# Attention, soft MoE and feed-forward on one core: a written order for SyncE's DMAs, and the maxima one step after the scores

## The chip, the cores and the metric

The kernel runs on one core of one Trainium2 chip. Its engines are TensorE (PE in the profile; PEld is its weight load), VectorE (DVE), ScalarE (ACT), GpSimd (POOL) and SyncE (SP), which issues nearly all DMAs (SPq in the rows). Each engine works through its own list of instructions in order, and they meet at semaphores. The metric is the device time of one execution in microseconds, and the time shown for a kernel is the median of its runs.

## The reference

Three layers follow one another; the change touches the first.

```python
scores = scale * np.matmul(q, k.transpose(0, 1, 3, 2))      # q, k, v: 8 x 8 x 576 x 64
scores = np.where(block_i >= block_j, scores, -1e9)         # causal by blocks of 64
scores = scores - np.max(scores, axis=-1, keepdims=True)
attn = np.exp(scores); attn = attn / (attn.sum(-1, keepdims=True) + 1e-9)
x = np.matmul(attn, v)                                      # then reshaped to 4608 x 512
logits = x @ phi                                            # soft MoE, 8 experts x 4 slots
slot_out[e] = np.maximum(slot_input[e] @ w1[e], 0) @ w2[e]  # slot_input: softmax over tokens
y = softmax(logits, axis=1) @ slot_out
out = np.maximum(y @ w_in, 0) ** 2 @ w_out                  # feed-forward, 4608 x 512
```

## The kernel before

Attention goes over 8 batches of 8 heads. Two heads make a pair, four pairs a batch, so there are 32 pairs, numbered n = 0 to 31 through all batches (bn is the batch, jn the pair in it). The work is pipelined over pairs, and `pair(n)` writes one step of that pipeline:

- `split(n + 3)` scales q and k of the pair three ahead into 16-bit high and low parts. ScalarE makes the high part (`high`), VectorE the low one (`low`). `prep_k` sends both parts of k through a DMA transpose to `s1` (in the rows s<-ka); q's high part is turned by TensorE (`turn_q`) and copied to `t1`; q's low part goes to `qb`.
- `maxpass(n + 2)` computes the scores of the pair two ahead in one pass for their row maxima alone: seven chunks, each a few matmuls into a PSUM tile ps_max and a VectorE reduction to pm. Its last part, `fin`, joins them, writes the maxima into `qb` (the last instruction is L535) and sends `qb` through a DMA transpose to `t2` (t<-qb, L540).
- `s2copy(n + 1)` is a DMA inside the core: it copies the upper half of s1 to a second tile s2 (s<-s, L952). There are two such tiles, used in turn.
- `scores(n)` computes the scores proper in seven chunks into ps_sc: each with s1 and t1, then with s2 and t2, which brings in the low part and the maxima. ScalarE takes the exponential of each chunk (p, L594; the last, small chunk gives pd, L576). The end of a pair, below, is the matmul of its last chunk (L574).
- `pv(n - 1)` multiplies the exponentials of the pair before with v, and sums them. GpSimd adds for it (ss).
- `aux` holds `scale`, the sums of squares that give the scaling: ScalarE squares k and q of a pair (junk, L380), TensorE sums over partitions (ps_ssq, L387), VectorE works out the scales. In odd pairs it does this for the pairs four and five ahead.
- `work` holds the soft MoE's part for the batch before (logits, running maxima, tokens), and `decq` the decoding of w_in, which comes as 64-bit numbers: 16 blocks, each loaded to raw (`load_in`), one ScalarE and four VectorE instructions a block (L185 to L206).

A pair is written in eight slots. Before, slot i holds chunk i of the scores and, right behind it, chunk i of the maxima; slot 0 holds also the pair's first steps of split, chunks 5 and 6 of the maxima and the output products.

DMA issues wait in a list `dq`, from which `loads(LR)`, with LR = 4, takes up to four in each slot. Loads of q and k come by pair (`load_pair`) for batches 0 and 1 and by batch (`load_batch`: first the small tails of k and q, then k, then q) after that; v by pair (`load_v`). `s2copy(n + 1)` is put at the head of `dq` in slot 2, and most loads at its head too:

```python
if i == 2 and n + 1 < N:
    dq.insert(0, lambda: s2copy(n + 1))
loads(LR)
```

In the whole of attention only TensorE keeps the order in which its instructions are written (`manual_schedule(engines={PE})`). On the other engines a scheduler orders them when the program is built, SyncE among them, so that the order of the DMAs is not that of `dq`.

Weights of the experts go into buffers that attention frees, by `wchunks`; the last of them only when attention ends. After attention come the experts and then the feed-forward.

Of the kernel before, what the change touches and what calls it, by code (L numbers as in the profile page):

```python
# [23 lines left out]
def tile_attn_soft_moe_ffn(  # L24
# [13 lines left out]
    B, H, S, D = q.shape  # L38
# [7 lines left out]
    NU = S // 128  # L46
# [38 lines left out]
    tin = tin_p.tile([128, KD, FF], F32, name="tin")  # L85
# [154 lines left out]
    def attention():  # L240
# [22 lines left out]
        N = B * NJ  # L263
# [40 lines left out]
        def load_v(n):  # L304
            b, j = divmod(n, NJ)
            t = v_tile(n)

            def main(hp):
                nc.sync.dma_start(
                    out=t[:, 0:NU, hp, :], in_=v[b][NJ * hp + j, 0:128 * NU, :].rearrange("(u p) d -> p u d", p=128)  # L310
                )

            def tail(hp):
                nc.sync.dma_start(
                    out=v_tail(b)[64 * hp:64 * hp + 64],
                    in_=v[b][NJ * hp:NJ * hp + NJ, 128 * NU:S, :].rearrange("j i d -> i j d"),
                )

            return [lambda: main(0)] + [lambda hp=hp: tail(hp) for hp in range(2) if j == 0] + [lambda: main(1)]

        def load_phi(hp):
            nc.sync.dma_start(
                out=phi2[64 * hp:64 * hp + 64, :, NSL * hp:NSL * hp + NSL],
                in_=phi.rearrange("(hp j p) s -> hp p j s", hp=2, p=64)[hp],
            )
# [25 lines left out]
        def load_batch(b):  # L351
            t = qk_tile(b)

            def main(nm, u):
                nc.sync.dma_start(
                    out=t[nm][:, 2 * u:2 * u + 2].rearrange("p x j d -> p (x j) d"),
                    in_=dict(q=q, k=k)[nm][b][:, 128 * u:128 * u + 128, :].rearrange("h p d -> p h d"),
                )

            def tail(nm, hp):  # L360
                nc.sync.dma_start(
                    out=t[nm][64 * hp:64 * hp + 64, 2 * NU],
                    in_=dict(q=q, k=k)[nm][b][NJ * hp:NJ * hp + NJ, 128 * NU:S, :].rearrange("j i d -> i j d"),
                )

            return [
                [lambda nm=nm, hp=hp: tail(nm, hp) for nm in "kq" for hp in range(2)],
                [lambda u=u: main("k", u) for u in range(NU)],
                [lambda u=u: main("q", u) for u in range(NU)],
            ]  # L370

        sc = {}
# [558 lines left out]
        raws = {}  # L931
# [8 lines left out]

        def decode_in(i):
            a, c = i % KD, i // KD
            return decode(dec_p, tin[:, a, 512 * c:512 * c + 512], raws.pop(i), 512)

        AHEAD, LR = 3, 4
        dq = load_pair(0, dict(q=nc.scalar)) + load_pair(1, dict(q=nc.scalar)) + load_pair(2) + load_pair(3)

        def loads(k):
            for _ in range(min(k, len(dq))):
                dq.pop(0)()  # L950
# [4 lines left out]
        with tc.manual_schedule(engines={mybir.EngineType.Activation}):  # L955
# [12 lines left out]
            m0 = maxpass(0)  # L968
            for f in m0[6:] + m0[:6] + [sp2[0], sp2[1], sp2[3]]:
                f()  # L970
        dq += load_v(0) + load_pair(4) + load_v(1) + load_pair(5) + [lambda hp=hp: load_phi(hp) for hp in range(2)]
        s3 = scale([AHEAD])
        m1 = maxpass(1)
        for i, f in enumerate(m1[6:] + m1[:6]):
# [7 lines left out]
        work, aux, decq, nraw = [], [], [], [0, 0]  # L982
        NRAW = KD * FF // 512
        ew = early = late_ = last = half = None
        bl = []
        def pair(n):
            nonlocal dq, work, aux, decq, bl, ew, early, late_, last, half
            bn, jn = divmod(n, NJ)
            m = maxpass(n + 2) if n + 2 < N else []
            s = scores(n) if n < N else []  # L990
            w = pv(n - 1) if n >= 1 else []
            if jn == 1:
                if bn >= 1:
                    work += batch(bn - 1)
                if bn + 1 == B:
                    while decq:
                        decq.pop(0)()
                    assert nraw[1] == NRAW, nraw
                    st_in.close()
                    wpools["a"] = w_st.enter_context(tc.tile_pool(name="wa", bufs=2, side="right"))  # L1000
                dq += wchunks({B - 2: 1, B - 1: 2}.get(bn, 0))

            elif jn == 2:
                if n == N - 2:
                    st_a.close()
                    wpools["e"] = w_st.enter_context(tc.tile_pool(name="we", bufs=1, side="right"))
                dq += wchunks({B - 2: 1, B - 1: 2}.get(bn, 0))
            elif jn == 3:
                if bn + 1 == B:
                    early, late_, last = batch(bn)  # L1010
                    work += early
                    st_b.close()
                    st_m.close()
                    wpools["m"] = w_st.enter_context(tc.tile_pool(name="wm", bufs=1, side="right"))
                    wpools["o"] = w_st.enter_context(tc.tile_pool(name="wo", bufs=2, side="right"))
                    dq += wchunks(3)
            elif n == N:
                work += late_
                st_c.close()
                wpools["n"] = w_st.enter_context(tc.tile_pool(name="wn", bufs=1, side="right"))  # L1020
                dq += wchunks(1)
            if nraw[1] < nraw[0] - 1 or NRAW == nraw[0] > nraw[1]:
                decq += decode_in(nraw[1])
                nraw[1] += 1
            if len(decq) <= 5 and 6 <= n and nraw[0] < NRAW:
                dq.append(lambda i=nraw[0]: load_in(i))
                nraw[0] += 1
            if n == 6:
                ew = wchunks(2)
            if n >= 7 and ew:  # L1030
                dq.append(ew.pop(0))
            if n + 2 < N:
                at = len(dq) if n < 4 else 0
                dq[at:at] = load_v(n + 2)
            if n == 0:
                dq += load_pair(6)
            if n == 1:
                dq[0:0] = load_pair(7)
            if jn == 1 and bn + 2 < B:
                bl = load_batch(bn + 2)  # L1040
                dq[len(load_pair(7)) if n == 1 else 0:0] = bl.pop(0) + bl.pop(0)
            if jn == 2 and bl:
                dq[0:0] = bl.pop(0)
            if n == 1:
                aux += scale([4]) + scale([5])
            if n == 2:
                aux += scale([6])
            if n % 2 and n > 1:
                ns = [i for i in (n + AHEAD + 1, n + AHEAD + 2) if i < N]
                aux += scale(ns, 2) if ns else []  # L1050
            sp = split(n + AHEAD) if n + AHEAD < N else []
            slot = {}

            def at_(i, *fs):
                slot.setdefault(i, []).extend(f for f in fs if f)

            get = lambda fs, i: fs[i] if i < len(fs) else None
            for i in range(7):
                at_(i, get(s, i), get(m, i) if i < 6 else None)
                if i == 0:  # L1060
                    early_ = sp and n != 1
                    at_(0, get(sp, 0) if early_ else None, get(m, 6), get(w, 0), get(sp, 1) if early_ else None, get(w, 1))
                    at_(0, get(sp, 2) if early_ else None)
            at_(3, get(w, 2))
            if n == 1:
                at_(3, sp[2])
                at_(4, sp[0])
                at_(7, sp[1], sp[3])
            else:
                at_(4, get(sp, 3))  # L1070
            for i in range(8):
                for f in slot.get(i, []):
                    f()
                if i == 2 and n + 1 < N:
                    dq.insert(0, lambda: s2copy(n + 1))
                loads(LR)
                f = aux.pop(0) if aux else None
                if f:
                    f()
                elif decq and i % 8:  # L1080
                    decq.pop(0)()
                for _ in range((i in (1, 3, 4, 6, 7)) if n < N - 3 else 1 if n < N - 1 else 2):
                    if work:
                        work.pop(0)()
            if n == N - AHEAD - 1:
                dq += wchunks(2)
            if n == N - 1:
                half = wchunk(14)
                dq += half[:1]
            if n >= 1:  # L1090
                P.pop(n - 1)
                T.pop(n - 1)
        with tc.manual_schedule(engines={mybir.EngineType.PE}):
            for n in range(N + 1):
                pair(n)
            nxt[0] += 1
            for f in dq + work + half[1:] + last:
                f()
# [585 lines left out]
```

## Time and profile before

| | |
|---|---|
| runs | 898.87, 904.22, 904.10 us; median 904.1 |
| the profiled execution | 901.67 us, its span 899.9 |
| before pair 0 ends | 0 to 39.95 us |
| pairs 1 to 31 | 39.95 to 435.2 us |
| rest of soft MoE, experts | 435.2 to about 505 us |
| feed-forward | about 505 to 899.9 us |
| DMA | 113.17 MB, 126 GB/s over the span |

All times in rows are of the profiled execution, counted from the start of its span; the 1.8 us between the span and its time lie outside. An engine's busy time says nothing by itself: it is compared with the length of its own stretch, pair by pair. The granted clock is a share of TensorE's full speed; it has two levels, 1.0 (2.4 GHz) and 0.5 (1.2 GHz), and a value between is a mean of the two over the stretch.

### The profile page before, as it was taken

To read this page: it belongs to the slowest core of one execution; us is meant where nothing else is said; L and a number is where in the kernel's file an instruction comes from. 1 tells how busy PE (TensorE), PEld (TensorE's weight loads), DVE (VectorE), ACT (ScalarE), POOL (GpSimd) and SP (SyncE) were. 2 spreads that over 40 slices of the span, in tenths; PEclk is the share of its full clock that TensorE was granted. 3 is DMA by queue.
4 is the path that set the end of the run, shared out by engine and by line. 5 is a ranking of instruction groups with operands and counts; after the bars stand their busy time and mean duration, and the time that the engine had idled before them with its cause. 6 is when DMAs were issued, how large, how long until landed. Compare 5 with 4: busy or idle time off the path is not lost.

```text
span 899.9 us, 21874 instructions
## 1 busy us (share of the span) xinstructions
PE 831.6 (92%) x8788; PEld 614.9 (68%) x8788; DVE 668.6 (74%) x1600; ACT 627.2 (70%) x1012; POOL 254.8 (28%) x394
## 2 busy tenths in 40 slices
PE   2778999898999989997997799999999999999998
PEld 1445667665676757664733344788888888888887
DVE  5755688888788878963551899888887888888881
ACT  5476788686878767753312689987878888888870
POOL 0234756557584846755200000000000000000000
PEclk9888999999999989999999799999999999999999
DMA  8899979879897969576999700100001000000002
GB/s 164 174 188 199 212 133 177 166 140 184 143 192 130 184 132 215 109 174 204 309 371 380 308 0 1 47 24 25 25 24 48 24 25 25 24 25 24 25 24 48
DMA packets 220486, 113.17 MB, mean 126 GB/s; under 512 B 192224, under 2 KB 194272, under 8 KB 220384
## 3 DMA queue, kind: packets, MB, share of 16 engines
q1 hardware_dynamic: 217728, 111.11, 53.7%
q8 instruction: 69, 1.13, 0.5%
q10 hardware_dynamic: 2656, 0.66, 0.4%
q14 instruction: 33, 0.27, 0.1%
HBM read 78.71 MB, written 9.44 MB: 98 GB/s over the span
## 4 chain that ended last, share of the span: by engine, by line
PE 64%; DMA 11%; POOL 8%; ACT 8%; DVE 4%; SPq 3%; issue 3%; ACTq 0%; DVEq 0%
PE ps_y L1498 14%; PE ps_x L1498 9%; PE ps_z L1498 9%; PE xm L629 6%; PE po L1520 4%; POOL ss L599 4%; DMA s<-s 4%; POOL ul L739 3%; PE ps_hb L1462 3%; PE ps_sc L556 3%; DMA wch<-in_moe_w_dram 3%; DMA ar_hi<-in_v_dram 2%; ACT p L594 2%; PE tl L640 2%; ACT t L465 1%
## 5 line engine op out<-in xcount | busy, mean ns | idle before, releaser
L1498 PEld LDWEIGHTS <-ah 128*128 128x128 f16 x1792 | 170.3, 98 | 21.9
L594 ACT ACTIVATE p<-ps_sc,es 128x512 f32<-128x512 f32 x192 | 128.9, 696 | 51.2 <-PE ps_sc L556 34.4
L491 DVE TENSOR_REDUCE pm<-ps_max 128x4 f32<-128x512 f32 x160 | 108.5, 683 | 58.2 <-PE ps_max L485 57.9
L1431 DVE TENSOR_TENSOR al<-a,ah 128x1024 f16<-128x1024 f32 (+1 forms) x128 | 138.5, 1124 | 16.7 <-ACT ah L1485 15.3
L599 POOL TENSOR_TENSOR ss<-p 128x384 f32<-128x384 f32 (+1 forms) x128 | 95.0, 763 | 176.4 <-ACT p L594 176.0
L556 PE MATMUL ps_sc<-t,s 128*128 128x512 f16 (+3 forms) x512 | 107.4, 302 | 21.3 <-DMA s<-s 11.4
L1485 ACT CAST ah<-a 128x1024 f16<-128x1024 f32 (+1 forms) x128 | 114.4, 936 | 15.0 <-DVE a L1431 13.6
L1591 POOL TENSOR_TENSOR ot<-u,p 128x256 f32<-128x256 f32 x16 | 12.5, 782 | 374.7 <-DVE u L1562 339.3
L1498 PE MATMUL ps_y<-bh,ah 128*128 128x256 f16 x384 | 104.9, 273 | 0.0
L1498 PE MATMUL ps_y<-bl,ah 128*128 128x256 f16 x384 | 104.7, 273 | 0.0
L1498 PE MATMUL ps_y<-bh,al 128*128 128x256 f16 x384 | 104.7, 273 | 0.0
L599 POOL TENSOR_TENSOR ss<-ss,p 128x320 f32<-128x320 f32 (+1 forms) x128 | 101.2, 791 | 11.8 <-ACT p L594 3.1
L629 PE MATMUL xm<-p,ar_hi 128*64 128x256 f32 (+3 forms) x512 | 97.6, 481 | 0.0
L1353 ACT ACTIVATE r<-ps_hb,alpha 128x1024 f32<-128x1024 f32 x64 | 71.1, 1112 | 34.1 <-PE ps_hb L1462 33.4
L1498 PEld LDWEIGHTS <-al 128*128 128x128 f16 x896 | 87.5, 98 | 10.1
L1431 DVE TENSOR_TENSOR a<-a 128x256 f32<-128x256 f32 x192 | 76.1, 424 | 3.9
L1498 PE MATMUL ps_x<-bh,ah 128*128 128x256 f16 x256 | 70.1, 274 | 0.0
L1498 PE MATMUL ps_z<-bh,ah 128*128 128x256 f16 x256 | 70.0, 273 | 0.0
L1498 PE MATMUL ps_z<-bh,al 128*128 128x256 f16 x256 | 69.8, 273 | 0.0
L1498 PE MATMUL ps_z<-bl,ah 128*128 128x256 f16 x256 | 69.8, 273 | 0.0
L1498 PE MATMUL ps_x<-bh,al 128*128 128x256 f16 x256 | 69.8, 273 | 0.0
L1498 PE MATMUL ps_x<-bl,ah 128*128 128x256 f16 x256 | 69.8, 273 | 0.0
(255 smaller groups left out, 1827.4 us busy)
## 6 DMA issues: line engine op xcount, KB each, us to landing
wch<-in_moe_w_dram SPq DMA_DIRECT2D x18, 1024.0 KB, 11.3
ar_hi<-in_v_dram SPq DMA_DIRECT2D x64, 128.0 KB, 3.6
raw<-in_moe_w_in_dram SPq DMA_DIRECT2D x16, 512.0 KB, 5.1
out_dram<-ot SPq DMA_DIRECT2D x32, 256.0 KB, 2.3
ar_hi<-in_moe_w_dram SPq DMA_DIRECT2D x6, 1024.0 KB, 9.3
s<-s SPq DMA_DIRECT2D x32, 144.0 KB, 3.3
wo<-in_moe_w_out_dram SPq DMA_DIRECT2D x4, 1024.0 KB, 8.7
ar_lo<-in_k_dram SPq DMA_DIRECT2D x12, 256.0 KB, 4.2
```

What stands on the lines that cost most here:

```text
L491: nc.vector.tensor_reduce(out=o, in_=i, axis=AX.X, op=ALU.max)
L556: nc.tensor.matmul(ps[:, c0:c0 + w].rearrange("p (s c) -> p s c", c=128), kk[:, 2 * t + hp, :], qq[:, 2 * u0 + hp:8:2, :], start=(c0 == 0 ...
L594: exps[:] = [nc.scalar.activation(out=pt, in_=ps, func=AF.Exp, scale=es[:, 0:1])]
L599: add = lambda o, x, y: nc.gpsimd.tensor_tensor(out=o, in0=x, in1=y, op=ALU.add)
L629: nc.tensor.matmul(box["xm"][64 * hp:64 * hp + 64, 128 * t:512], vs[:, t, hp, :], r, start=(t == 0), stop=(t == 3),)
L739: add = lambda o, x, y: nc.gpsimd.tensor_tensor(out=o, in0=x, in1=y, op=ALU.add)
L1353: nc.scalar.activation(out=r[:, c0:c1], in_=ps[:, c0:c1], func=AF.Relu, **kw)
L1431: sub = lambda o, a, b: nc.vector.tensor_tensor(out=o, in0=a, in1=b, op=ALU.subtract)
L1462: nc.tensor.matmul(ps[:, 512 * j + 256 * a:512 * j + 256 * a + 256], ws[:, 128 * f:128 * f + 128], ctt[:, c0:c0 + 256], start=True, stop=True,
L1485: nc.scalar.copy(v(hl[n % 2][0][:, 2 * kq:2 * kq + 2], s), v(a7[n, kq], s))
L1498: nc.tensor.matmul(acc[:, 0:HM], a[:, k], b[:, k], start=bool(first and k + j == 0), stop=(k == KH - 1 and j == 2), skip_group_check=not f ...
L1520: nc.tensor.matmul(pos[t], g[:, 512 * a + 128 * t:512 * a + 128 * t + 128], tt[:, c, a], start=(c == 0 and a == 0), stop=(c == KH - 1 and ...
```

## The change

- SyncE joins TensorE among the engines that keep the written order.
- `s2copy(n + 1)` is written first in pair n, not put into `dq` in slot 2.
- Loads are taken three in slot 0, ahead of the slot's other work, one in each of slots 1 to 5, two in 6 and 7; all are put at the end of `dq`, in the order v, k of the batch after next (pair 1 of a batch), q (pair 2).
- Batch 1 is loaded by `load_batch`, all of k and then all of q, ahead of the second pair's v.
- Chunk i of the maxima stands in slot i + 1, behind chunk i + 1 of the scores; chunks 5 and 6 in slot 1; `fin` in slot 6. Slot 0 has no maxima.
- Block i + 2 of w_in is loaded by an entry behind block i's decode, and a decode joins `decq` in each pair from 7 on where there is room.

```diff
             return [
-                [lambda nm=nm, hp=hp: tail(nm, hp) for nm in "kq" for hp in range(2)],
-                [lambda u=u: main("k", u) for u in range(NU)],
-                [lambda u=u: main("q", u) for u in range(NU)],
+                [lambda hp=hp, nm=nm: tail(nm, hp) for hp in range(2)] + [lambda u=u, nm=nm: main(nm, u) for u in range(NU)]
+                for nm in "kq"
             ]
...
-        dq += load_v(0) + load_pair(4) + load_v(1) + load_pair(5) + [lambda hp=hp: load_phi(hp) for hp in range(2)]
+        dq += load_v(0) + load_batch(1)[0] + load_batch(1)[1] + load_v(1) + [lambda hp=hp: load_phi(hp) for hp in range(2)]
...
+            if n + 2 < N:
+                dq += load_v(n + 2)
+            if jn in (1, 2) and bn + 2 < B:
+                dq += load_batch(bn + 2)[jn - 1]
...
             for i in range(7):
-                at_(i, get(s, i), get(m, i) if i < 6 else None)
+                at_(i, get(s, i))
                 if i == 0:
...
+                else:
+                    at_(i, get(m, i - 1), get(m, 6) if i == 1 else None)
...
+            if n + 1 < N:
+                s2copy(n + 1)
             for i in range(8):
+                if i == 0:
+                    loads(3)
                 for f in slot.get(i, []):
                     f()
-                if i == 2 and n + 1 < N:
-                    dq.insert(0, lambda: s2copy(n + 1))
-                loads(LR)
+                if i:
+                    loads(2 if i > 5 else 1)
...
-        with tc.manual_schedule(engines={mybir.EngineType.PE}):
+        with tc.manual_schedule(engines={mybir.EngineType.PE, mybir.EngineType.SP}):
```

SyncE before, in pairs 9 and 10, from the transpose of pair 11's t2 on; s_0_141 and s_1_142 are the two s2 tiles, so the L952 rows are the s2copies of pairs 11 and 12, s_2665 is s1 of pair 13:

```order
L355 DMA ar_lo<-in_q_dram 128x8x64 x3
L540 DMA_TRANSPOSE t_2618<-qb_140 128x9x128
L309 DMA ar_hi<-in_v_dram 128x4x64
L314 DMA ar_hi<-in_v_dram 64x4x64
L452 DMA_TRANSPOSE s_2665<-ka 128x9x128
L314 DMA ar_hi<-in_v_dram 64x4x64
L936 DMA raw<-in_moe_w_in_dram 128x1024
L309 DMA ar_hi<-in_v_dram 128x4x64
L952 DMA s_1_142<-s_2191 64x1152
L309 DMA ar_hi<-in_v_dram 128x4x64 x2
L952 DMA s_0_141<-s_2395 64x1152
```

The same place after; s_1_142<-s_2187 is pair 11's s2copy, t_2874 is pair 12's t2, s_0_141<-s_2395 is pair 12's s2copy:

```order
L956 DMA s_1_142<-s_2187 64x1152
L309 DMA ar_hi<-in_v_dram 128x4x64
L314 DMA ar_hi<-in_v_dram 64x4x64 x2
L451 DMA_TRANSPOSE s_2661<-ka 128x9x128
L309 DMA ar_hi<-in_v_dram 128x4x64
L361 DMA ar_lo<-in_q_dram 64x4x64
L935 DMA raw<-in_moe_w_in_dram 128x1024
L361 DMA ar_lo<-in_q_dram 64x4x64
L355 DMA ar_lo<-in_q_dram 128x8x64 x2
L539 DMA_TRANSPOSE t_2874<-qb_138 128x9x128
L355 DMA ar_lo<-in_q_dram 128x8x64 x2
```

Pair 11's s2copy has moved from behind the transpose of pair 13's s1 to ahead of it and of the whole pair's loads; pair 12's now follows the transpose of pair 12's t2, two parts of q, a weight part and raw.

ScalarE before, in pair 11, from the second exponential to the last; d are two small exponentials of the soft MoE, the two junk rows on ar_lo square k and q of pair 16:

```order
L594 ACTIVATE p<-ps_sc,es 128x512
L817 ACTIVATE d<-d 128x128
L380 ACTIVATE junk,ssq<-ar_lo 128x576
L594 ACTIVATE p<-ps_sc,es 128x512
L380 ACTIVATE junk,ssq<-ar_lo 128x576
L594 ACTIVATE p<-ps_sc,es 128x512 x2
L576 ACTIVATE pd<-ps_sc,es 128x128
```

The same pair after:

```order
L593 ACTIVATE p<-ps_sc,es 128x512
L379 ACTIVATE junk,ssq<-ar_lo 128x576
L815 ACTIVATE d<-d 64x32
L816 ACTIVATE d<-d 128x128
L593 ACTIVATE p<-ps_sc,es 128x512 x2
L185 ACTIVATE dec_sq<-raw 128x512
L593 ACTIVATE p<-ps_sc,es 128x512
L575 ACTIVATE pd<-ps_sc,es 128x128
L379 ACTIVATE junk,ssq<-ar_lo 128x576
```

The squaring of q has moved from ahead of the last two exponentials p to behind pd.

## Rows read from the trace of the kernel before

**Rows 1.** Busy time by stage: stretch, length, busy us (instructions), clock, DMA share, GB/s.

```profile
39.95:95.18 55.23, 44.26 (x572) 27.49 (x570) 30.16 (x98) 37.44 (x78) 23.92 (x33) 0.88 1.05 200
...
130.05:333.93 203.88, 192.82 (x2617) 134.11 (x2615) 167.78 (x466) 150.28 (x313) 128.01 (x192) 0.97 0.89 160
333.93:435.20 101.27, 94.46 (x1271) 67.12 (x1269) 71.31 (x209) 62.08 (x123) 59.87 (x97) 0.98 0.78 183
435.20:505.00 69.80, 59.20 (x593) 26.50 (x590) 32.24 (x129) 20.11 (x47) 4.83 (x8) 0.97 1.01 362
```

**Rows 2.** The same by pair, from end to end; busy: PE, PEld, DVE, ACT, POOL.

```profile
118.67:130.05 11.38, 11.14 (x165) 7.67 (x163) 8.89 (x26) 9.39 (x24) 6.01 (x9) 1.00 0.65 146
...
165.97:180.93 14.96, 12.99 (x166) 8.46 (x164) 11.54 (x31) 9.40 (x24) 6.22 (x9) 0.89 0.73 139
180.93:192.07 11.14, 11.14 (x166) 7.22 (x164) 8.23 (x26) 8.82 (x17) 4.93 (x7) 1.00 0.65 133
192.07:204.11 12.04, 11.93 (x168) 9.09 (x166) 10.98 (x28) 10.48 (x23) 9.33 (x15) 1.00 0.97 174
...
216.85:231.99 15.14, 13.12 (x166) 8.53 (x163) 11.54 (x31) 9.40 (x24) 6.23 (x9) 0.89 0.71 142
...
267.91:280.52 12.61, 11.46 (x166) 7.88 (x163) 11.54 (x31) 9.51 (x24) 6.22 (x9) 1.00 0.81 151
316.42:333.93 17.51, 14.07 (x166) 8.78 (x164) 11.64 (x31) 9.40 (x24) 6.22 (x9) 0.81 0.73 134
...
406.54:423.20 16.66, 12.62 (x146) 8.10 (x144) 5.82 (x22) 6.58 (x14) 8.38 (x16) 0.90 0.67 191
423.20:435.20 12.00, 11.22 (x152) 8.45 (x149) 6.12 (x19) 4.94 (x9) 4.91 (x9) 1.00 0.85 267
```

**Rows 3.** Waits from 95 to 435 us: total us, times, longest.

```profile
PE ps_sc L556 <- DMA s<-s: 9.3, 3, 4.0
```

**Rows 4.** SyncE's issues in order of time in pair 10: start, us.

```profile
153.59 2.09 SPq L355 DMA_DIRECT2D ar_lo<-in_q_dram  x3
...
162.25 0.55 SPq L936 DMA_DIRECT2D raw<-in_moe_w_in_dram  x1
...
163.32 1.34 SPq L952 DMA_DIRECT2D s<-s  x1
```

**Rows 5.** TensorE in order of time, start of pair 11; in brackets the wait ahead.

```profile
169.09 0.39 PE L556 MATMUL ps_sc<-t,s 128*128 128x512 f16 x1 [1.81 <-DMA ar_hi<-in_v_dram]
```

**Rows 6.** The chain that ended last, in order of time: start, us.

```profile
400.81 11.10 DMA s<-s
```

**Rows 7.** The line of s2copy, all 32.

```profile
DMA to landing us min/median/max: 2.3/3.3/11.1
```

**Rows 8.** SyncE's issues in order of time, end of pair 2.

```profile
67.41 0.51 SPq L952 DMA_DIRECT2D s<-s  x1
```

**Rows 9.** TensorE in order of time, pairs 2 and 3.

```profile
56.87 0.58 PE L477 MATMUL ps_max<-s,t 128*128 128x128 f16 x2 [1.92 <-DMA s<-ka]
...
70.82 0.46 PE L556 MATMUL ps_sc<-t,s 128*128 128x512 f16 x1 [2.02 <-DMA s<-s]
```

**Rows 10.** Waits from 39.95 to 95.18 us.

```profile
PE ps_ssq L387 <- ACT junk L380: 4.1, 4, 2.3
```

**Rows 11.** VectorE in order of time: last instruction of the maxima, pairs 10 and 12.

```profile
170.83 0.19 DVE L535 SCALAR_TENSOR_TENSOR qb<-ps_max,qb 128x9 f16<-128x9 f32 x1
...
197.58 0.20 DVE L535 SCALAR_TENSOR_TENSOR qb<-ps_max,qb 128x9 f16<-128x9 f32 x1
```

**Rows 12.** The line of a pair's last exponential: ns min/median/max, first and last start.

```profile
L576 ACT ACTIVATE pd<-ps_sc,es x32: 358/362/420, 40.7 to 436.0; 128x128 f32<-128x128 f32 x32
```

**Rows 13.** The line of the squarings, those on ar_lo.

```profile
L380 ACT ACTIVATE junk<-ar_lo x32: 669/682/721, 8.9 to 330.3; 128x576 fp8e4<-128x576 f32 x32
```

**Rows 14.** The line of the transpose to t2, its issues.

```profile
L540 SPq DMA_TRANSPOSE t<-qb x32: 1272/1871/3552, 30.5 to 410.9; - x32
```

**Rows 15.** SyncE's own waits, the whole span.

```profile
SPq L540 <- DVE qb L535: 13.1, 8, 3.7
```

More of the change, by code (lines that the diff above doesn't have):

```diff
@@ L942, in decode_in, with load_next @@
             a, c = i % KD, i // KD
-            return decode(dec_p, tin[:, a, 512 * c:512 * c + 512], raws.pop(i), 512)
-        AHEAD, LR = 3, 4
+            def load_next():
+                load_in(i + 2)
+            fs = decode(dec_p, tin[:, a, 512 * c:512 * c + 512], raws.pop(i), 512)
+            return fs + [load_next] if i + 2 < NRAW else fs
+        AHEAD = 3
         dq = load_pair(0, dict(q=nc.scalar)) + load_pair(1, dict(q=nc.scalar)) + load_pair(2) + load_pair(3)
@@ L984, in attention, with dec_step @@
         ew = early = late_ = last = half = None
-        bl = []
+        def dec_step():
+            if isinstance(decq[0], int):
+                decq[0:1] = decode_in(decq[0])
+            decq.pop(0)()
+            if decq and getattr(decq[0], "__name__", "") == "load_next":
+                decq.pop(0)()
         def pair(n):
-            nonlocal dq, work, aux, decq, bl, ew, early, late_, last, half
+            nonlocal dq, work, aux, decq, ew, early, late_, last, half
             bn, jn = divmod(n, NJ)
@@ L996, in pair @@
                     while decq:
-                        decq.pop(0)()
-                    assert nraw[1] == NRAW, nraw
+                        dec_step()
+                    assert nraw[0] == NRAW, nraw
                     st_in.close()
@@ L1021, in pair @@
                 dq += wchunks(1)
[L1022 to L1027, printed above, removed]
+            if n + 2 < N:
+                dq += load_v(n + 2)
+            if jn in (1, 2) and bn + 2 < B:
+                dq += load_batch(bn + 2)[jn - 1]
             if n == 6:
                 ew = wchunks(2)
[L1030 to L1043, printed above, removed]
+                dq += [lambda i=i: load_in(i) for i in range(2)]
+            if n >= 7:
+                if ew:
+                    dq.append(ew.pop(0))
+                if len(decq) <= 6 and nraw[0] < NRAW:
+                    nraw[0] += 1
+                    decq.append(nraw[0] - 1)
             if n == 1:
@@ L1058, in pair @@
             for i in range(7):
-                at_(i, get(s, i), get(m, i) if i < 6 else None)
+                at_(i, get(s, i))
                 if i == 0:
                     early_ = sp and n != 1
-                    at_(0, get(sp, 0) if early_ else None, get(m, 6), get(w, 0), get(sp, 1) if early_ else None, get(w, 1))
+                    at_(0, get(sp, 0) if early_ else None, get(w, 0), get(sp, 1) if early_ else None, get(w, 1))
                     at_(0, get(sp, 2) if early_ else None)
+                else:
+                    at_(i, get(m, i - 1), get(m, 6) if i == 1 else None)
             at_(3, get(w, 2))
@@ L1080, in pair @@
                 elif decq and i % 8:
-                    decq.pop(0)()
+                    dec_step()
                 for _ in range((i in (1, 3, 4, 6, 7)) if n < N - 3 else 1 if n < N - 1 else 2):
```

## The prediction

> **What bounds the kernel now.** I read the stretches of the span by stage first, then the pairs of attention one by one, and only then the waits. The stage table shows where TensorE is not busy: pairs 1 to 4 of attention (39.95 to 95.18 us) hold 44.26 us of its work in 55.23, at a mean granted clock of 0.88; pairs 8 to 23 hold 192.82 in 203.88; pairs 24 to 31 hold 94.46 in 101.27 [rows 1]. The stage behind attention (435.20 to 505.00) moves 362 GB/s with the DMA engines busy throughout [rows 1]: it is bound by weights, whose buffers attention frees, so it should start earlier by what attention saves. The feed-forward stage from 505 us on is not touched. So the change is decided in the 395 us of pairs 1 to 31.
>
> The pair table shows a pattern. A pair that nothing holds up takes 11.14 to 11.38 us (those ending at 192.07 and 130.05); the last pair of each batch takes 14.96, 15.14, 12.61 and 17.51 (ending at 180.93, 231.99, 280.52, 333.93), three of them at a clock of 0.81 to 0.89 [rows 2]. TensorE's waits name the cause: the second matmul of a pair's first scores chunk waits for the transfer s<-s, which is s2copy [rows 3]. In pair 11 it starts at 169.09 after a wait of 1.81 us [rows 5]; the profile names the v transfer there, which landed last, but what the matmul reads is the s2copy issued at 163.32 [rows 4]. That copy needs only s1, which exists well before, and the end of the scores that used the same s2. It is late because SyncE stands before it, with q, transposes, raw and v. An s2copy takes 2.3 us at best, 3.3 in the median and 11.1 at worst [rows 7]; the worst lies on the chain of waits at 400.81 [rows 6], behind megabytes of weights.
>
> **The change part by part.** No compute instruction is added or removed. What moves is order: on SyncE and TensorE as written, on ScalarE and VectorE through the scheduler.
>
> *First term, pairs 1 to 4.* Before, pair 2's maxima for pair 4 waited 1.92 us for s<-ka, and pair 3's first scores 2.02 us for their s2copy [rows 9], issued at 67.41 [rows 8], less than a microsecond before pair 3 began. After, that s2copy stands at the start of pair 2, and the maxima stand behind the output products, so that both transfers have a cover. Whole loading takes 12 issues for batch 1 instead of 20. The bound above is all idle time and all lost clock: 10.97 us idle (55.23 less 44.26) and 12% of 55.23, 6.6 us [rows 1], together 17.6. The bound below is nothing, since the DMA engines are already busy (share 1.05 [rows 1]) and pair 4 now needs the whole of its batch, not its own quarter. I take the length of pair 7, 11.38 us [rows 2], for each: 55.23 - 4 x 11.38 = 9.7. Against this, TensorE still waits for a sum of squares in pair 1, up to 2.3 us as before [rows 10], since the last part of q is now issued behind the transposes of pairs 0 to 3, and pair 3 pays cost (a) below, 1.0. Term: 9.7 - 2.3 - 1.0 = **6 us**.
>
> *Second term, pairs 8 to 23.* If s2copy lands in time, the four last pairs fall to 11.38: 3.6 + 3.8 + 1.2 + 6.1 = 14.7 us [rows 2]; this holds the lost clock too. Three costs stand against it.
>
> (a) The squaring of q for the pair five ahead now stands behind the pair's last exponential on ScalarE, in pairs 3, 11, 15, 19 and 23, and TensorE's sum of squares follows directly on the last scores. Price: 0.36 for that exponential [rows 12] and 0.68 for the squaring [rows 13], 1.04 us of TensorE idle; four times here, 4.2 us. Below it could be nothing, where TensorE would wait for VectorE anyway.
>
> (b) Decodes come once in nearly every pair from 8 to 23, not in three of four. A pair without one shows 8.23 us of VectorE work, a pair with one 10.98 to 11.54 [rows 2], so the fourth pair of a batch goes from 8.23 to about 11.2, in a length of 11.14: VectorE is then as full as TensorE. Bounds: 0 (absorbed) to 3 us a batch; I take 0.6, 2.4 in all, since a pair with 10.98 us of VectorE work has 11.93 of TensorE work in 12.04 [rows 2], little lost.
>
> (c) SyncE's own waits now stand in the written order. The transpose of t2 waits for the maxima, whose last instruction came 4.9 us after the end of pair 10 (170.83 [rows 11] against 165.97); written a step later, I estimate 5 to 7. Behind it stand, at the end of each batch's third pair, two parts of q, in most batches a weight part, raw, and only then the next s2copy. A transpose takes 1.9 us of issue [rows 14], the others 0.5 to 0.7 each [rows 4], together 4.1; to land s2copy takes 3.3 [rows 7] to the 5.8 of pair 11 (163.32 to 169.09). That is 12.4 to 16.9 us after the pair's end. It is needed at 13.7: 11.38, 1.04 of (a), and 1.3 from the last scores to that matmul (165.97 to 167.28, where its wait began). So 0 to 3.2 us, four times; I take 1, 4 in all. Everywhere else s2copy stands nearly a pair ahead of its use. Term: 14.7 - 4.2 - 2.4 - 4 = **4 us**, bounds -14 and +15.
>
> Here a rule of the Trainium skill speaks against the change. The row shows that SyncE waited for the last instruction of the maxima eight times, 3.7 us at the longest [rows 15]. DMA: Bandwidth & Descriptors, section Anatomy of one DMA (told there of GpSimd's path), says that DMA engines do not wait on semaphores: "any semaphore wait happens on the issuing sequencer before dispatch". By that rule a fixed order makes each late producer hold every transfer written behind it, and the time would be that of the slower rival below; the row bears it out for single waits, not for a whole order.
>
> *Third term, pairs 24 to 31.* Pair 30 lasted 16.66 us, the next 12.00 [rows 2], and its s2copy took 11.1 behind weights [rows 6, 7]. After, that copy stands at the start of pair 29 ahead of those weights: 4.7 us. No decode is left by then, which relieves VectorE in pairs 24 to 28, I estimate by half of what (b) costs: 1.2. Term: **6 us**, bounds 4 and 8. Two weight parts of 0.25 MB are loaded later than before, while the DMA engines have room (share 0.78 [rows 1]); if they had not, 0.5 MB at 362 GB/s is 1.4 us.
>
> Sum: 6 + 4 + 6 = 16 us. Against the profiled execution's 901.7 that gives 886; that execution lies 2.4 below the median of the runs, 904.1, from which it would be 888. I forecast **887**.
>
> **The rivals.** *Nothing much changes.* The DMA engines, not their order, limit pairs 1 to 4 (share 1.05), which then give 3 us; (a) to (c) eat the second term; the end gives 5. That is 8 us: 896. For it: VectorE and TensorE are both nearly full. Against it: the stalls have one visible cause, which the order removes.
>
> *Slower.* The one mechanism is that the t2 transpose blocks SyncE. If the maxima end later than about 8 us after the pair's end, t2, the rest of q and s2copy land behind their use at two pair starts of each batch, the first and the third. A stall of that kind costs 3.7 us (14.7 / 4), twice in six batches: 44, with (a) and (b) 52; against that stand 14.7 + 9.7 + 6 = 30. It would be 22 us slower, 926. For it: in the first pair of a batch the maxima already ended 5.5 us late (197.58 against 192.07 [rows 2, 11]). Against it: there s2copy follows the transpose directly, and 5.5 + 1.9 + 0.5 + 3.3 is within the 12.04 of the next pair.
>
> *The change doesn't do what it says.* If s2copy, though written early, had to wait on SyncE for scores that end late, nothing would be gained but the third term: 898. Against it: it is written directly behind the scores it waits for. I count it with the first rival.
>
> *More than forecast.* All stalls go, the clock stays full, and the costs hide behind each other: 15 + 14 + 7 = 36 us, 868.
>
> **How the numbers follow.** Chances: forecast (870 to 895) 0.60, more than that 0.08, nothing much 0.20, slower 0.12. For eight in ten the range runs from 868 to 906. What a measurement can tell from no change is taken as 1%, 9 us: faster by more 0.66, within it 0.23, slower 0.11.
>
> **What would show it.** In the profile after: no wait of TensorE for s<-s in the last pair of a batch nor at the start of pair 30, pairs 1 to 4 near 11 us at a clock near 1, a new wait of ps_ssq for junk of about 1 us once a batch, VectorE near 11 us in each pair from 8 to 23, and the weights' stage earlier by what attention saves, at the same length. The forecast is wrong if waits for s<-s or t<-qb reappear at the first or third pair of a batch, if pairs 1 to 4 still wait for q or k, or if the saved time is lost again in the weights' stage.

## The result, and the profile after

The changed kernel takes 906.6 us in the median of 15 runs, the kernel before 901.2 in 15; the ratio is 1.0056 (95% interval 1.003 to 1.0083). The change is slower by half a per cent; 16 us less had been forecast. The profiled execution took 903.58 us (span 901.7), 1.9 more than that of before.

By stage, after (columns as in [rows 1]); the stretches are those of [rows 1], cut at the same events, with pairs 8 to 23 from 126.04 to 337.47:

```profile
40.58:90.86 50.28, 42.85 (x570) 27.41 (x569) 31.38 (x101) 37.69 (x78) 22.41 (x31) 0.90 0.89 162
126.04:337.47 211.43, 192.97 (x2615) 131.97 (x2613) 178.59 (x480) 156.05 (x317) 129.62 (x193) 0.98 0.92 173
337.47:434.67 97.20, 93.03 (x1269) 65.86 (x1267) 62.76 (x193) 61.05 (x120) 55.22 (x97) 1.00 0.80 174
434.67:505.00 70.33, 61.18 (x590) 26.30 (x587) 30.86 (x128) 19.07 (x45) 3.93 (x8) 0.93 1.03 378
```

Pairs 1 to 4 are 5.0 us shorter than in [rows 1] and pairs 24 to 31 are 4.1 shorter, but pairs 8 to 23 are 7.6 longer. Attention ends at 434.67, half a microsecond sooner. The pairs themselves (columns as in [rows 2]): pairs 11, 23 and 30, then the four pairs of batch 3, then the first pairs of batches 2, 4, 5 and 6:

```profile
167.76:178.78 11.02, 11.02 (x164) 7.72 (x163) 11.02 (x31) 9.89 (x23) 6.07 (x9) 1.00 1.09 209
326.46:337.47 11.01, 11.01 (x164) 7.71 (x162) 11.01 (x31) 9.52 (x23) 6.06 (x9) 1.00 0.72 151
411.56:422.43 10.87, 10.87 (x144) 7.61 (x143) 6.34 (x22) 6.55 (x14) 8.00 (x15) 1.00 1.16 304
178.78:194.78 16.00, 13.07 (x164) 7.68 (x163) 11.32 (x32) 9.77 (x20) 5.10 (x8) 0.89 1.10 239
194.78:207.14 12.36, 12.25 (x166) 9.00 (x165) 11.09 (x26) 10.36 (x24) 9.05 (x15) 1.00 0.43 98
207.14:220.81 13.67, 12.27 (x168) 8.75 (x167) 11.51 (x36) 9.06 (x17) 12.27 (x20) 1.00 1.21 196
220.81:231.82 11.01, 11.01 (x163) 7.71 (x162) 11.01 (x31) 9.88 (x23) 6.07 (x9) 1.00 1.08 204
126.04:141.74 15.70, 13.13 (x165) 7.61 (x163) 10.08 (x31) 9.91 (x20) 4.71 (x8) 0.89 1.09 223
231.82:247.02 15.20, 11.63 (x164) 7.21 (x163) 11.35 (x32) 9.77 (x20) 5.12 (x8) 1.00 1.17 189
284.06:300.44 16.38, 13.02 (x164) 7.64 (x163) 11.43 (x32) 9.77 (x20) 5.10 (x8) 0.90 0.88 176
337.47:351.81 14.34, 11.45 (x164) 7.22 (x163) 8.72 (x28) 9.27 (x18) 4.70 (x8) 1.00 0.75 122
```

What was to gain was gained: the last pairs take 11.0 us instead of 14.96, 15.14, 12.61 and 17.51 [rows 2], 16.2 in all, and pair 30 takes 5.8 less. But the first pairs, 11.14 us before [rows 2], now take 14.34 to 16.38: 77.6 for the five shown, 21.9 more than five times 11.14. Third pairs rose from 12.74 (204.11 to 216.85 in [rows 2]) to 13.67 and second ones from 12.04 to 12.36: 5.0 in all over pairs 8 to 23.

TensorE's waits in pairs 8 to 23 name the new stall (columns as in [rows 3]):

```profile
PE ps_ssq L386 <- ACT junk L379: 8.5, 4, 3.4
PE ps_max L476 <- DVE pm L490: 4.9, 4, 1.2
PE ps_sc L555 <- DMA s<-s: 3.9, 2, 2.4
```

The chain that ended last, at the start of pair 12, says why the squares come late (start, us; its last rows):

```profile
176.03 0.24 SPq L539
176.32 0.59 SPq L355
176.95 4.02 DMA ar_lo<-in_q_dram
181.16 0.79 ACT junk L379 x2
181.98 0.59 PE ps_ssq L386 x2
```

ScalarE's row for that square of q, with its wait in brackets:

```profile
181.16 0.68 ACT L379 ACTIVATE junk<-ar_lo 128x576 fp8e4<-128x576 f32 x1 [1.40 <-DMA ar_lo<-in_q_dram]
```

And SyncE's issues in pair 11:

```profile
170.96 2.04 SPq L355 DMA_DIRECT2D ar_lo<-in_q_dram  x2
173.11 3.16 SPq L539 DMA_TRANSPOSE t<-qb  x1
176.32 1.26 SPq L355 DMA_DIRECT2D ar_lo<-in_q_dram  x2
177.62 0.64 SPq L169 DMA_DIRECT2D ar_hi<-in_moe_w_dram  x1
178.35 0.38 SPq L935 DMA_DIRECT2D raw<-in_moe_w_in_dram  x1
178.78 0.53 SPq L956 DMA_DIRECT2D s<-s  x1
```

On VectorE the last instruction of those maxima:

```profile
172.86 0.18 DVE L534 SCALAR_TENSOR_TENSOR qb<-ps_max,qb 128x9 f16<-128x9 f32 x1
```

Read from the end: TensorE stood still for 2.93 us until the square of q was summed; the square waited for the last part of q, which was issued at 176.95 because two of its four large parts stand behind the transpose of t2. In pair 11 SyncE came to that transpose at 173.0, just when VectorE was done with the maxima (173.04), so it hardly waited there; but the issue kept it until 176.27. The chain gives the transpose only the last 0.24 us of this, because a matmul of the scores ended at 176.03; whether the issue waited for that matmul or was merely slow is not shown. (By the program, the tile that it writes was last read by the scores of pair 10, done at 168.04.) In pair 15 it is a wait and an issue:

```profile
223.00 1.77 SPq L355 DMA_DIRECT2D ar_hi<-in_q_dram  x2
226.16 2.23 SPq L539 DMA_TRANSPOSE t<-qb  x1
228.44 1.22 SPq L355 DMA_DIRECT2D ar_hi<-in_q_dram  x2
```

SyncE stood idle for 1.4 us and issued for 2.23. In pairs 19 and 23 it was 1.2 and 2.34, 2.3 and 1.30: in each of the four pairs the rest of q came 3.3 to 3.6 us later than without that transpose ahead of it.

Of SyncE's own waits the one that [rows 15] shows has grown from 13.1 us, 3.7 at the longest, to:

```profile
SPq L539 <- DVE qb L534: 81.7, 16, 10.8
```

This row has one releaser, and rows of other releasers can count the time of the issue itself as a wait. Taken from SyncE's rows in order of time, as the gap between the end of one issue and the start of the next, its idle time ahead of the transposes of t2 is 30 us before and 90 after. Yet its idle time in all, up to 460 us, fell from 151 to 129. So it isn't the amount of waiting that makes the loss, but what stands behind it.

Behind attention, the feed-forward's first matmul starts 1.7 us later than before although attention ends 0.5 sooner (its line in before, then after: ns min/median/max, first and last start):

```profile
L1462 PE MATMUL ps_hb<-cts,ws x256: 277/282/682, 540.9 to 866.3; 128*128 128x256 f32 x128
```

```profile
L1469 PE MATMUL ps_hb<-cts,ws x256: 278/281/684, 542.6 to 868.2; 128*128 128x256 f32 x128
```

### The profile page after: what moved, and what is told of

It is laid out like the page before. It is cut to its first block, busy times and chain, and to the rows that moved or that the text cites. A ratio compares the mean times of both kernels' runs of the same rounds, so it can differ in the third digit from the quotient of the medians.

```text
span 901.7 us, 21791 instructions
## 1 busy us (share of the span) xinstructions
PE 833.1 (92%) x8788; PEld 612.3 (68%) x8788; DVE 673.2 (75%) x1600; ACT 633.4 (70%) x1012; POOL 251.2 (28%) x394
## 4 chain that ended last, share of the span: by engine, by line
PE 70%; DMA 10%; POOL 7%; ACT 5%; SPq 2%; DVE 2%; issue 2%; ACTq 0%; POOLq 0%
PE ps_y L1505 14%; PE ps_x L1505 9%; PE ps_z L1505 9%; PE xm L628 6%; PE ps_sc L555 5%; POOL ss L598 5%; PE po L1527 4%; PE ps_hb L1469 3%; DMA s<-s 3%; PE ps_u L729 2%; POOL ul L738 2%; DMA ar_lo<-in_q_dram 2%; PE ps_h L1196 2%; PE ps_x L833 2%; PE ps_max L476 2%
## 5 line engine op out<-in xcount | busy, mean ns | idle before, releaser
L598 POOL TENSOR_TENSOR ss<-p 128x384 f32<-128x384 f32 (+1 forms) x128 | 87.8, 704 | 176.2 <-ACT p L593 175.9
L598 POOL TENSOR_TENSOR ss<-ss,p 128x320 f32<-128x320 f32 (+1 forms) x128 | 104.4, 816 | 16.4 <-ACT p L593 8.6
L628 PE MATMUL xm<-p,ar_hi 128*64 128x256 f32 (+3 forms) x512 | 89.9, 450 | 0.0
## 6 DMA issues: line engine op xcount, KB each, us to landing
wch<-in_moe_w_dram SPq DMA_DIRECT2D x18, 1024.0 KB, 13.1
```

The costliest lines, as they stand in the source:

```text
L598: add = lambda o, x, y: nc.gpsimd.tensor_tensor(out=o, in0=x, in1=y, op=ALU.add)
L628: nc.tensor.matmul(box["xm"][64 * hp:64 * hp + 64, 128 * t:512], vs[:, t, hp, :], r, start=(t == 0), stop=(t == 3),)
```

## The experiments

My theory (A) was that SyncE's fixed order holds the last of q, and the next s2copy, behind the transpose of t2. The rivals were B, that VectorE is too full with a decode in every pair, and C, that it is ScalarE's order alone, as priced in the prediction. Each ratio below is to the kernel before in the same session, where its median lay between 900.6 and 904.4 us; differences in us are between medians, and a few us of them are noise.

**q ahead of v.** In the changed kernel:

```diff
-            if n + 2 < N:
-                dq += load_v(n + 2)
             if jn in (1, 2) and bn + 2 < B:
                 dq += load_batch(bn + 2)[jn - 1]
+            if n + 2 < N:
+                dq += load_v(n + 2)
```

> The changed kernel with one edit: in the second and third pair of a batch the loads of k and q for the batch after next are put into the list ahead of v, not behind it. Theory A (SyncE's fixed order: the last parts of q stand behind the transpose of t2, which waits for the maxima, so their squares and TensorE's sum of squares come late): the waits of ps_ssq for junk in pairs 12, 16, 20 and 24 (11.3 us) fall under 3, those pairs from 14.3-16.4 us to 12-13.5 (the s2copy, issued as late as before, may now show 0 to 2 us there); 893 to 900 us. Theory B (VectorE is too full with a decode in every pair; what TensorE waits for in the first pair only stands for that): first pairs stay over 14.5 us with another wait, 904 to 908 us. Theory C (ScalarE's order alone, at 1.04 us a time as forecast): 4 us less, 902.

Measured: 898.6 us, ratio to before 0.996 (0.9929 to 0.9991), 8 less than the changed kernel and in A's range. But the first pairs did not come to the 12 to 13.5 us that A gave, pair 24 (11.44) excepted, so that the range was met by luck. Another stall came out from under the first. TensorE at the start of pair 12, with the wait ahead in brackets, and the pair (columns as in [rows 2], but cut 0.3 us later, where the last matmul ends):

```profile
178.16 0.38 PE L386 MATMUL ps_ssq<-ssq,ones 128*128 128x4 f32 x2 [1.16 <-ACT junk L379]
183.54 0.39 PE L555 MATMUL ps_sc<-t,s 128*128 128x512 f16 x1 [3.23 <-DMA s<-s]
```

```profile
177.00:194.68 17.68, 13.29 (x163) 8.14 (x164) 10.32 (x32) 9.65 (x19) 5.12 (x8) 0.90 0.96 210
```

s2copy was as late in the changed kernel (issued at 178.78 there), and most of its lateness lay in the shadow of the squares. C is not borne out: in the changed kernel the square waited for the transfer of q, 1.40 us, and not for ScalarE.

**s2copy ahead of the transpose.** Only this, in the changed kernel:

```diff
-            if n + 1 < N:
-                s2copy(n + 1)
+            if n == 0:
+                s2copy(1)
...
                 else:
+                    if i == 6 and n + 2 < N:
+                        at_(6, lambda: s2copy(n + 2))
                     at_(i, get(m, i - 1), get(m, 6) if i == 1 else None)
```

> The changed kernel with one edit: s2copy(n+2) is written in slot 6 of pair n, behind the last scores and ahead of the transpose of t2, instead of s2copy(n+1) first in pair n. Theory A: the waits for s<-s (2.2, 2.4 and 1.5 us in pairs 3, 8 and 16) go, the ps_ssq waits of pairs 12, 20 and 24 stay; 900 to 904 us. Theory B: no change, 904 to 908. A rival (the late s2copy is what costs, the wait for the squares lies in its shadow): first pairs fall to about 12, 890 us.

Measured: 901.2 us, 0.9983 (0.9951 to 1.0016). No wait for s<-s is left in pairs 8 to 24; those for the squares are (pair 12 shown):

```profile
181.07 0.38 PE L386 MATMUL ps_ssq<-ssq,ones 128*128 128x4 f32 x2 [2.79 <-ACT junk L379]
```

The same pair, cut as above:

```profile
178.28:194.11 15.83, 13.04 (x163) 7.61 (x164) 11.52 (x32) 9.76 (x19) 5.10 (x8) 0.89 1.08 225
```

The first pairs of batches 2 to 5 sum to 63.3 us in the changed kernel, to 65.4 with q ahead of v and to 62.2 here (a trace of the slowest of this kernel's ten runs). The single edits' 8 and 5 us did not come from these pairs.

**Both.** The two edits together.

> The changed kernel with both edits: k and q ahead of v in the list, and s2copy(n+2) ahead of the transpose of t2. Theory A: neither the squares nor s2copy are late; the first pairs of a batch come to 11.2-12.5 us, the last pairs stay at 11.0, so about 5 x 3.5 = 17 us and 2 for pair 3 are gained: 886 to 892 us. Theory B: above 900 us, first pairs over 14.

Measured: 879.1 us, 0.9739 (0.9681 to 0.9797), 27 less than the changed kernel where the single edits gave 8 and 5, and below A's range. The four pairs of batch 3:

```profile
173.88:186.00 12.12, 11.62 (x165) 7.26 (x163) 10.50 (x32) 9.61 (x20) 5.26 (x8) 1.00 1.20 218
186.00:198.31 12.31, 11.92 (x167) 8.87 (x165) 11.18 (x26) 10.14 (x24) 7.73 (x14) 1.00 0.57 155
198.31:211.98 13.67, 12.27 (x169) 8.75 (x168) 11.51 (x36) 9.04 (x17) 12.27 (x20) 1.00 1.22 203
211.98:222.99 11.01, 11.01 (x164) 7.71 (x163) 11.01 (x30) 9.88 (x23) 6.06 (x9) 1.00 1.16 216
```

The first pair is down to 12.12 us at a clock of 1.00, and the first pairs of batches 2 to 5 sum to 47.3. The DMA engines are as busy there (share 1.20) as in the slow first pairs (0.75 to 1.17), so it is not their load that made those slow. SyncE's order is still fixed, and it still stands idle ahead of the transposes of t2, 51 us in all. Two transfers were late behind the same transpose, and either alone held the pair.

**Fewer decodes.** In the changed kernel:

```diff
-                if len(decq) <= 6 and nraw[0] < NRAW:
+                if len(decq) <= 6 and nraw[0] < NRAW and jn != 3:
```

> The changed kernel with one edit: no block of w_in is put into the list of decodes in the last pair of a batch, so that three pairs of four take one, as before the change. Theory A: the waits of ps_ssq for junk in the first pairs stay (over 9 us in sum); 902 to 907 us, within 4 of the changed kernel. Theory B: VectorE's relief takes the first pairs from 15-16 to about 12.5 us and the 1.2 us wait for pm in the third pairs away; 890 to 895 us.

Measured: 909.5 us, 1.0087 (1.0053 to 1.0121), slightly above A's range. In pair 12 VectorE's work fell from 11.3 to 8.7 us, the pair still took 14.5:

```profile
180.30:194.80 14.50, 11.62 (x164) 7.21 (x163) 8.73 (x25) 9.64 (x19) 4.79 (x7) 1.00 0.99 201
```

The first pairs of batches 2 to 5 still sum to 62.2. The 1.2 us waits for pm in the third pairs stayed as well, so decodes are not their cause. B is out.

**SyncE left to the scheduler.** All else as changed:

```diff
-        with tc.manual_schedule(engines={mybir.EngineType.PE, mybir.EngineType.SP}):
+        with tc.manual_schedule(engines={mybir.EngineType.PE}):
```

> The changed kernel, but SyncE doesn't keep the written order; the scheduler orders its DMAs again. All else is as changed. Theory A (the fixed order holds q and s2copy behind the transpose of t2): in the order built here the last parts of q and the next s2copy stand behind one transpose of s1 and not behind that of t2; first pairs come to 12-13.5 us, the ps_ssq waits of the first pairs fall under 4 us in sum; 888 to 898 us. If something else of the change is what costs: 903 us or more.

Measured: 878.4 us, 0.974 (0.9674 to 0.9806), 28 less than the changed kernel and better than A's range. All of pairs 8 to 23:

```profile
122.15:315.67 193.52, 187.61 (x2612) 130.63 (x2612) 175.02 (x480) 154.47 (x317) 130.82 (x192) 1.00 1.00 186
```

They take 193.5 us, not 211.4. SyncE stands idle ahead of the transposes of t2 for 24 us, and for 133 in all up to 460 us, no less than in the changed kernel (129); but in pairs 10 and 11 the large parts of q stand ahead of that transpose, and TensorE waits nowhere from 120 to 355 us for the squares or s<-s. So one line of the change costs more (28 us) than all the rest brings (23).

**The old code with a fixed order.** The opposite edit in the kernel before, SP added to the engines that keep the order.

> The kernel before with one edit: SyncE keeps the written order too. If the fixed order by itself is what costs (each wait of SyncE for a transpose's producer holds q, s2copy and the transposes of s1 written behind it): waits for s<-ka, s<-s and the squares together grow by 15 us or more over those before; 910 to 930 us. If the order costs only together with the new places of the loads: 895 to 905 us.

Measured: 1025.0 us, 1.1355 (1.1305 to 1.1406), far over what I expected. TensorE waits 76.3 us for s<-s (16 times, 10.3 at the longest) and SyncE itself waits for the buffer of raw, and nearly as long (77.5 us) for k to be split ahead of the transposes of s1:

```profile
SPq L936 <- DVE tin L206: 80.5, 10, 13.4
```

That wait was 32.9 us in the kernel before, where the scheduler places those loads. The changed text writes each such load behind the decode that frees its buffer, and there all waits of that line are 2.0 us. I take this to be one reason why the fixed order cost 28 us there and 124 here; it was not tried apart from the rest.

**The old code with an early s2copy.** In the kernel before, no other edit:

```diff
+            if n + 1 < N:
+                s2copy(n + 1)
             for i in range(8):
                 for f in slot.get(i, []):
                     f()
-                if i == 2 and n + 1 < N:
-                    dq.insert(0, lambda: s2copy(n + 1))
```

> The kernel before with one edit: s2copy(n+1) is written first in pair n, not put into the list in slot 2; the scheduler still orders SyncE. If the gain that was forecast for the last pairs comes from s2copy alone and costs nothing elsewhere: pairs 11, 15, 19 and 23 fall from 15.0, 15.1, 12.6 and 17.5 to 11.2-12.5 us and pair 30 from 16.7 to 11-12, the first pairs stay at 11.1; 880 to 890 us. If the late copy is not the cause: 898 to 904 us.

Measured: 879.5 us, 0.9743 (0.9684 to 0.9802). Pairs 11, 12 and 30:

```profile
158.72:170.53 11.81, 11.17 (x166) 8.09 (x164) 11.54 (x31) 9.51 (x24) 6.21 (x9) 1.00 0.78 146
170.53:181.67 11.14, 11.14 (x167) 7.22 (x164) 8.22 (x26) 8.82 (x17) 4.93 (x7) 1.00 0.64 132
386.77:398.15 11.38, 11.16 (x146) 7.58 (x144) 5.82 (x22) 6.58 (x14) 8.39 (x16) 1.00 0.90 245
```

The gain forecast from s2copy is real, and this edit alone has it without the fixed order: pair 11 falls by 3.2, pair 30 by 5.3, and pair 12 stays at 11.14. The time lies just under the expected range.

**Maxima in their old slots,** first in the changed kernel, then with both edits of above (there `fin` stays in slot 6). The cut leaves out that chunks 5 and 6 go back to slot 0:

```diff
-                at_(i, get(s, i))
+                at_(i, get(s, i), get(m, i) if i < 6 else None)
...
-                else:
-                    at_(i, get(m, i - 1), get(m, 6) if i == 1 else None)
```

> The changed kernel with the maxima in their old slots: chunk i behind chunk i of the scores, chunks 5 and 6 in slot 0, the transpose to t2 in slot 5. If the shift only costs: the 1.2 us waits of ps_max for pm in the third pairs of a batch go, third pairs come back from 13.66 to 12.74 and second ones from 12.36 to 12.05 (about 5 us in all), and t2, q and s2copy are issued a good microsecond sooner, so that the first pairs lose 0 to 1 us each: 897 to 902 us. If the shift is what gives its cover to the transposes: last pairs go from 11.0 back over 12, or waits for s<-ka come back; 907 to 915 us.

> The kernel with k and q ahead of v and s2copy ahead of the transpose of t2, and with the chunks of the maxima in their old slots (chunks 5 and 6 in slot 0); the transpose to t2 stays in slot 6. If the shift of the maxima only costs there too: third pairs 12.74 instead of 13.66, second 12.05 instead of 12.36, about 5 us: 871 to 877 us. If it gives cover: 880 to 888 us.

Measured: 923.4 us, 1.0226 (1.0156 to 1.0295), and 906.8, 1.0054 (1.0016 to 1.0092): 17 and 28 more than the same kernels with the maxima a step late, and in both above what I had expected of either case. A wait of TensorE from 40 to 440 us, in the second of them:

```profile
PE ps_max L476 <- DMA s<-ka: 26.8, 14, 5.4
```

With both edits and late maxima the same wait is 1.6 us in all; in the first of them it is 16.1, where the changed kernel has none. So the shift gives the transposes of s1 their cover where SyncE is fixed. It also makes third pairs longer: in the changed kernel with old slots pair 14 took 12.8 us, not 13.67.

**Towards a better kernel.** Three kernels with SyncE scheduled: the one above with k and q ahead of v; the old code with early s2copy and batch 1 loaded whole; and the first of these with late maxima in pairs 0 to 4 only (the cut is of this one, without the line for chunks 5 and 6).

```diff
+                late = n < 5
+                at_(i, get(s, i), get(m, i) if i < 6 and not late else None)
...
-                else:
+                elif late:
                     at_(i, get(m, i - 1), get(m, 6) if i == 1 else None)
```

> The changed kernel with SyncE ordered by the scheduler and with k and q ahead of v in the list. If the 3.3 us wait of ps_ssq in pair 4 that was left there comes from q of batch 2 being issued late: that pair falls from 14.5 to 10-11.5 us and the time to 873 to 876 us. If the scheduler's order doesn't follow the list, or s2copy gets late for it: 877 to 884 us.

> The kernel before with s2copy written first in pair n, and with batch 1 loaded whole as in the changed kernel; the scheduler orders SyncE. If whole loading is what shortened pairs 1 to 3 in the changed kernel with a scheduled SyncE (31.7 us there, 38.2 with loads by pair): 873 to 876 us. If it makes q of batch 1 late: a wait for the squares of 2 us or more in pairs 1 or 4, 878 to 884 us.

> The changed kernel with SyncE ordered by the scheduler, k and q ahead of v in the list, and the maxima a step late in pairs 0 to 4 only, in their old slots from pair 5 on. If the late maxima help only at the start, where the transposes of s1 have no other cover, and cost 0.7 us a batch later (48.4 us for four pairs against 47.7 with the old slots): 3 to 4 us less than with the shift throughout, 871 to 874 us. If the old slots bring back waits for s<-ka in that order of SyncE: 876 us or more.

Measured: 875.6 us, 0.9709 (0.9667 to 0.9752); 879.1, 0.974 (0.9705 to 0.9774); 875.5, 0.9689 (0.965 to 0.9728). The first has the expected time for another reason: pair 4 still takes 14.2 us, since the wait for the squares fell to 0.63 and one of 2.17 for s<-s took its place. The second gains nothing: pair 2 waits 5.09 us for s<-ka, a wait that neither case had named, though the time lies in the second case's range. The third is above its range. It ends attention 3.0 us sooner than the first (406.02 against 409.06), but not for the reason expected: pairs 8 to 23 give 0.4 us (193.45 against 193.85), since third pairs fall from 13.7 to 12.7 and first and last pairs grow from 11.2 to 12.0 and 11.8; the rest comes from pairs 1 to 7 and 24 to 31. And the feed-forward starts half a microsecond later (first the first kernel, then the third):

```profile
L1469 PE MATMUL ps_hb<-cts,ws x256: 278/281/684, 513.8 to 839.2; 128*128 128x256 f32 x128
```

```profile
L1470 PE MATMUL ps_hb<-cts,ws x256: 277/281/681, 514.3 to 839.7; 128*128 128x256 f32 x128
```

The weights' stage gave those 3 us back. With 2.9 to 3.1% less than before, these two have the lowest medians; they can't be told apart from each other, and their intervals overlap with that of the old code with an early s2copy.

## Why the prediction was wrong

*The gains* were right. Last pairs: 14.7 forecast, 16.2 measured. Pair 30: 4.7 and 5.8. Pairs 1 to 4: 6 and 5.0, with the wait for the squares in pair 1 that was allowed for, 2.99 us instead of 2.3. What failed is the second term, pairs 8 to 23: 4 us less were forecast, 7.6 more were measured. The third, pairs 24 to 31, gave 4.1 of 6, since pair 24 lost 3.2 in the same way.

*Cost (a) is the step that failed.* It took the squaring of q as a question of ScalarE's order, at 1.04 us of TensorE, four times. It did not ask when q would be there. The order shown in the part on the change has two large parts of q behind the transpose of t2, and cost (c) worked out for that very queue when s2copy could land, but for s2copy alone. The same sum for q goes so: the maxima end 5 to 7 us after the pair (5.0 measured: 173.04 against 168.04, the end of pair 10's last matmul), the transpose takes 1.9 (measured 3.16), one more part 0.6, and the last one lands 4.0 after its issue. Measured, with 0.2 for the gaps, that is 12.9 us after the pair's end; the square and its start take 1.0 more, and the sum of squares is due at 11.0. The waits were 2.93, 2.1, 3.4 and 2.9 us in pairs 12, 16, 20 and 24, and in pairs 12 and 20 the pair's mean clock fell to 0.89 and 0.90 as well: the same work of TensorE took 13.07 and 13.02 us there, 11.14 before.

*Cost (c)* was right in its bounds as a wait, 0 to 3.2 us a time, but taken as 1 and as a cost beside (a). It is an alternative to it: the late copy mostly hid behind the late squares, and came out at 3.2 when these were early. Where q was in time, in pair 8, it showed: its s2copy, issued at 123.56, landed 7.43 us later, where 3.3 to 5.8 had been reckoned with, and TensorE waited 2.40 us and lost 2.0 more by a clock of 0.89. Together (a) and (c) were put at 8.2 us; over pairs 8, 12, 16 and 20 they cost 18.7 (63.28 less four times 11.14), and pair 24 another 3.2.

*Cost (b)*, 2.4 us, stood for the wrong thing. Relief from decodes saved no time. Second and third pairs did lose 5.0, which stayed without those decodes; with the maxima in their old slots they were back at 11.75 and 12.74 (scheduled SyncE).

*The slower rival* had the mechanism, SyncE blocked by the transpose of t2, and its place at the first pairs, but a condition that proved needless (maxima over 8 us late; in pair 11 5.0 were enough) and twice the price: 44 us for stalls of this kind, at first and third pairs, where 21.9 were measured, at first pairs alone. The sentence from DMA: Bandwidth & Descriptors of the Trainium skill, section Anatomy of one DMA, that a wait sits on the issuing sequencer, was left to this rival as borne out "for single waits, not for a whole order". The trace agrees with it for the whole order too: in pairs 15, 19 and 23 q stood behind SyncE's idle time of 1.4, 1.2 and 2.3 us ahead of the transpose, besides the issue itself. What the rule leaves open is the price. With both edits the order is as fixed, SyncE stands idle ahead of those transposes longer than before the change (51 us, 30 before), and most of the loss in the first pairs is gone (47.3 us for four of them against 63.3, 44.6 before), since q and s2copy no longer stand behind them.

*The weights' stage* did not begin earlier, and ran 2.2 us later against attention's end (105.7 to 107.9 us from there to the first feed-forward matmul). I did not settle how much of this is weight parts that were issued later and how much its lower clock, 0.93 against 0.97 in [rows 1].

Half of the change helps: the early s2copy is worth 22 us by itself, and the fixed order of SyncE takes 28 from the whole.

## What to carry to other kernels

Before an engine that issues DMAs is put into a fixed order, list for each issue that can wait what stands behind it, and work out for every one of these, not for the one in view, when it lands and when its reader needs it. When one late transfer is repaired and the gain is small, look for the next one due just behind it: here two edits gave 8 and 5 us alone and 27 together. An early copy could be had by writing one line earlier, with the scheduler still in charge; the order didn't have to be fixed for it.

## What was not expected of the hardware

The transpose of t2 kept SyncE 1.2 to 3.7 us for its issue in the changed kernel (1.48 in the median of 32); with q and s2copy queued behind it, it took 3.16 in pair 11, 2.2 and 2.3 in pairs 15 and 19 and 1.3 in pair 23, where I had taken 1.9. Why it differs so is not shown. And a fixed order alone, on text that was not written for it, cost 124 us, with TensorE's mean clock down to 0.925 of full speed from 0.973.
